# Issuing the two expert weights behind V of batch 0 and V of batch 1 in a fused attention and feed-forward kernel

## The chip, the cores and the metric

The kernel runs on one core of one Trainium2 chip. The metric is the device time of one execution in microseconds (us). A time without a unit below is a point on the profile's time axis, in us from the start of the profiled span.

## The reference

Block-causal attention over 8 batches, 8 heads, 576 positions and head dimension 64 is followed by a feed-forward layer whose gate is `h * sigmoid(beta * h)`. All inputs and the output are float32.

```python
scores = q @ k.T / sqrt(64)                       # per batch and head, 576 x 576
scores = where(block_i >= block_j, scores, -1e9)  # blocks of 64 positions
attn = softmax(scores) @ v                        # 576 x 64
x = attn, heads side by side                      # 4608 x 512
h = x @ w_in                                      # w_in 512 x 2048
g = h * 1 / (1 + exp(-beta * h))
out = g @ w_out                                   # w_out 2048 x 512
```

## The kernel before

The kernel is written as a list of operations with dependencies, buffers and assumed durations. At build time a planner (`Plan.schedule`) plays this list through a model of the engines and writes down one fixed order for each engine; on the chip every engine works through its order and stops at an instruction whose semaphores have not come yet. The assumed durations (`xfer` of a DMA, `LAND` until a DMA counts as landed) and the priorities (`prio`, smaller first) set only the order. The dependencies (`deps`) become real waits.

**Attention.** A unit is one pair of heads of one batch, four units per batch. Q and K of a unit are loaded into staging buffers `ST` (six of them), cast to bf16 on POOL (`QKn`, two buffers, L493 for batches 0 and 1, L532 later) and transposed into `QKT` (three buffers): on the tensor engine PE for batches 0 and 1 (L502, copied out at L510), by DMA afterwards (L539). The score products are at L561 and their exponentials are taken on ACT (L569, L581) into `E` (three buffers). V of a whole batch is loaded into `Vs` (two buffers), cast on POOL to `Vn` (L447), and multiplied with E at L605, thirty matmuls per unit, called PV below. The result is divided by its sums on DVE (L617, L624) and transposed into `xT` (L649 and L659 or L657 up to batch 4, by DMA at L637 from batch 5).

**Feed-forward.** Nine row blocks of 512 rows, called row 0 to row 8. For each of 16 groups j, four matmuls at L695 (`w_in`) fill a PSUM bank, ACT takes a tanh (L705) and DVE forms `gT` (L709). Then L726 (`w_out`) sums over the 16 groups for four slices of the block, and ACT writes them out. For row 0 the first three slices are split into four parts, each needing only a quarter of w_out. `w_in` and `w_out` are each loaded in four pieces: 1 MB of float32 is read and 512 KB of bf16 is written, so these DMAs cast.

**Queues.** Q, K and V are issued on SP (queue q1 in the profile). The weights are issued on POOL between its casts (queue q0). All transfers run on the same 16 DMA engines.

**What held the weights and loads in this version** is a short block near the end: w_in piece 0 waits for Q and K of unit 3, the other pieces also for the second half of V of batch 0; w_out waits for Q and K of unit 6; and the Q and K of units 4 to 7 wait for w_in piece 1 to land.

```python
for i, w in enumerate(win):
    w.deps += [ld["Q", 3], ld["K", 3]] + (ld["V", 0, 4] if i else [])
for w in wout:
    w.deps += [ld["Q", 6], ld["K", 6]]
for u in range(4, 8):
    for o in [ld["Q", u], ld["K", u]] + (ld["V", 1, 0] if u == 4 else []):
        o.deps += [win[1]]
```

Of the kernel before, what the change touches and what calls it, by code (L numbers as in the profile page):

```python
# [9 lines left out]
B, H, S, D = 8, 8, 576, 64  # L10
# [19 lines left out]
class Op:  # L30
    def __init__(self, engs, dur, lat, emit, deps, tiles, prio, mode, dma, xfer):
        self.xfer = xfer
        self.engs, self.dur, self.lat, self.emit = engs, dur, lat, emit
        self.deps, self.tiles, self.prio, self.mode, self.dma = list(deps), tiles, prio, mode, dma
        self.eng = None
        self.start = self.end = None
        self.order = None
        self.need = False
        self.tick = None
        self.after = None  # L40
        self.lazy = False
        self.fill = 0


class Plan:
# [4 lines left out]
    SLACK = 120.0  # L50
    LAND = 2000.0
    BACKLOG = 4000.0
# [22 lines left out]
    def schedule(self):  # L75
# [17 lines left out]
        order = {e: [] for e in engs}  # L93
        now, nsched, rings = 0.0, 0, 0.0
        import heapq
        events = [0.0]
        pend = []
# [18 lines left out]
        fill = [o for o in self.ops if o.fill]  # L116
        while nsched < len(self.ops) - len(fill) or pend:
            if not events:
                raise RuntimeError("the plan has no way on")
            now = heapq.heappop(events)  # L120
            while pend and pend[0][0] <= now + 1e-9:
                _, _, o = heapq.heappop(pend)
# [20 lines left out]
            while progress:  # L143
                progress = False
                for e in engs:
# [4 lines left out]
                    for o in pool:  # L150
# [5 lines left out]
                        if o.after is not None and o.after.start is None:  # L156
                            continue
                        if o.lazy and rings > now + self.BACKLOG:
                            heapq.heappush(events, rings - self.BACKLOG + 1)
                            continue  # L160
# [50 lines left out]
                    heapq.heappush(pend, (o.end, o.idx, o))  # L211
                    heapq.heappush(events, o.end)
                    heapq.heappush(events, eng_free[e])
# [75 lines left out]
def bass_blockwise_causal_attn__then__act_swish_beta_kernel(  # L289
# [10 lines left out]
    with es:  # L300
# [97 lines left out]
        for a in range(4):  # L398
            def fwi(g, e, a=a):
                n = slice(512 * a, 512 * a + 512)  # L400
                return [g.dma_start(w_in[:, :, n], moe_w_in[:, n].rearrange("(c p) n -> p c n", p=128))]

            win.append(P.op("POOL", 1000, fwi, xfer=3400, dma=(f"d_win{a}", 1), prio=-19))
        for a in range(4):
# [3 lines left out]

            wout.append(P.op("POOL", 1000, fwo, xfer=3400, dma=(f"d_wout{a}", 1), prio=-18))

# [14 lines left out]
        for b in range(B):  # L425
            ts, t = P.tile("Vs"), P.tile("V")
            tl[b] = t
            for h0, h1 in ([(0, 4), (4, 8)] if b == 0 else [(0, 8)]):
                vs = []
                for i in range(6):  # L430
                    def fv(g, e, ts=ts, b=b, h0=h0, h1=h1, i=i):
                        if i < 4:
# [38 lines left out]
        for u in range(NU):  # L471
# [8 lines left out]
            if b < QB:  # L480

                turned = []
                for w, (nm, src) in enumerate((("Q", q), ("K", k))):
# [5 lines left out]

                    o = ld[nm, u] = P.op("SP", 420, fl, tiles=[ts], xfer=1200, prio=u, dma=["d_S", 0, 1])  # L490

# [324 lines left out]
```

## Time and profile before

| | |
|---|---|
| median of 3 runs | 376.37 us (375.22 to 379.33) |
| the profiled execution | 380.57 us, its span 378.8 us |
| PE busy | 345.8 us, 91% of the span |
| ACT, DVE, POOL busy | 212.3, 163.2, 75.9 us |
| read from and written to HBM | 36.71 MB and 9.44 MB |
| mean granted clock of PE | 0.963 |

The profiled execution is 1.77 us longer than its span and 4.2 us longer than the median run. PE is the engine with the most work, so time is to be looked for where PE stands still: a wait of another engine counts only where PE waits for it in turn. In the timelines an entry gives start, length, engine, line and operation, and in square brackets the idle time ahead of it with what ended it. An engine name ending in q (SPq) is its queue of DMA issues: the length is that of the issue, not of the transfer.

### The profile page before, as it was taken

The page shows a single profiled execution, that of the slowest core. Times are in us where ns is not written, and L with a number is a line of the kernel's source. Part 1 is how long each engine was busy: PE and PEld are TensorE (multiplying, and loading weights), DVE is VectorE, ACT ScalarE, POOL GpSimd, SP SyncE. Part 2 cuts the span into 40 slices and gives each one's busy share as a digit, 9 for nine tenths or more (in the row PEclk, how much of TensorE's full clock was granted, in tenths as well). Part 3 has the DMA queues.
Part 4 walks back from the last instruction along what each step waited for, and adds up shares of the span by engine and source line. Part 5 has one row for each costly group of instructions (what it writes and reads, how often), then busy time and mean ns, then how long its engine had stood idle before and what let it go on. Part 6 is the DMA issues. An engine that isn't in the chain of part 4 may idle for free.

```text
span 378.8 us, 6727 instructions
## 1 busy us (share of the span) xinstructions
PE 345.8 (91%) x2728; PEld 171.7 (45%) x2728; DVE 163.2 (43%) x367; ACT 212.3 (56%) x314; POOL 75.9 (20%) x105
## 2 busy tenths in 40 slices
PE   7779923999899799999999999999999999999986
PEld 4454403544354454454544544444554444444432
DVE  4556921416522365523864137314740750740710
ACT  2847840317934759647897189519932841742821
POOL 6451804323242241053003120400000000000000
PEclk9899985999999689999999999999999999999999
DMA  8969999989989987699066899870121002001002
GB/s 213 183 106 240 212 211 191 186 208 249 207 193 230 191 193 163 139 226 235 3 137 149 186 194 172 179 154 29 32 61 60 25 3 80 29 28 55 29 29 83
DMA packets 146527, 52.03 MB, mean 137 GB/s; under 512 B 134704, under 2 KB 141888, under 8 KB 146496
## 3 DMA queue, kind: packets, MB, share of 16 engines
q1 hardware_dynamic: 137088, 37.97, 49.3%
q10 hardware_dynamic: 5184, 9.44, 7.1%
q0 software_dynamic: 4224, 4.19, 7.0%
q8 instruction: 21, 0.34, 0.4%
q14 instruction: 10, 0.08, 0.1%
HBM read 36.71 MB, written 9.44 MB: 122 GB/s over the span
## 4 chain that ended last, share of the span: by engine, by line
PE 64%; SPq 7%; ACT 6%; DMA 3%; DVE 2%; issue 1%
PE PS L726 28%; PE PS L695 25%; PE PS L605 6%; SPq L521 4%; PE PS L561 4%; ACT E L569 3%; SPq L637 2%; ACT th L705 2%; DMA QKT<-QKn 2%; PE PS L649 2%; DVE gT L709 1%; DMA xT<-xq 1%; SPq L524 1%; SPq L436 0%; DVE xq L624 0%
## 5 line engine op out<-in xcount | busy, mean ns | idle before, releaser
L695 PE MATMUL PS<-xT,w_in 128*128 128x512 bf16 x576 | 133.7, 382 | 0.6 <-DVE gT L709 0.5
L709 DVE SCALAR_TENSOR_TENSOR gT<-th,PS 128x512 bf16<-128x512 f32 x144 | 97.5, 684 | 78.5 <-ACT th L705 77.9
L726 PE MATMUL PS<-w_out,gT 128*128 128x512 bf16 x576 | 128.4, 380 | 2.2 <-DVE gT L709 2.2
L705 ACT ACTIVATE th<-PS,beta 128x512 f32<-128x512 f32 x144 | 98.4, 700 | 24.6 <-PE PS L695 24.5
L569 ACT ACTIVATE E<-PS 128x1024 bf16<-128x1024 f32 x96 | 95.8, 1044 | 20.0 <-PE PS L561 19.7
L726 PEld LDWEIGHTS PS<-w_out,gT 128*128 128x128 bf16 x576 | 54.8, 98 | 69.0 <-DVE gT L709 3.2
L695 PEld LDWEIGHTS PS<-xT,w_in 128*128 128x128 bf16 x576 | 52.7, 98 | 65.8 <-issue 5.1
L737 ACT ACTIVATE ost<-PS 128x512 f32<-128x512 f32 x36 | 21.5, 597 | 97.5 <-PE PS L726 97.5
L605 PE MATMUL PS<-Vn,E 128*128 128x65 bf16 x960 | 37.9, 201 | 16.2 <-POOL Vn L447 14.9
L561 PE MATMUL PS<-QKT 64*128 64x512 bf16 (+5 forms) x384 | 40.6, 290 | 7.5 <-ACT E L569 5.5
L605 PEld LDWEIGHTS PS<-Vn,E 128*128 128x128 bf16 x960 | 35.7, 103 | 23.7 <-POOL Vn L447 13.4
L532 POOL CAST QKn<-ST 128x640 bf16<-128x640 f32 x48 | 34.7, 722 | 49.2 <-DMA ST<-in_k_dram 25.4
L447 POOL CAST Vn<-Vs 128x2560 bf16<-128x2560 f32 (+1 forms) x9 | 18.8, 2084 | 105.9 <-DMA Vs<-in_v_dram 105.9
L561 PEld LDWEIGHTS PS<-QKT 64*128 64x128 bf16 (+1 forms) x384 | 13.7, 96 | 31.1 <-issue 9.7
L624 DVE TENSOR_TENSOR xq<-PS,inv 128x640 bf16<-128x640 f32 x32 | 26.3, 822 | 0.9
L617 DVE RECIPROCAL inv<-PS 128x10 f32<-128x10 f32 x32 | 7.0, 219 | 44.5 <-PE PS L605 44.3
L575 DVE MEMSET E<- 64x64 uint32 x64 | 7.2, 112 | 38.0 <-ACT E L569 36.5
L659 DVE COPY xT<-PS 128x64 bf16<-128x64 bf16 (+2 forms) x40 | 9.6, 286 | 15.9 <-PE PS L649 15.8
L581 ACT ACTIVATE E<-PS 128x64 bf16<-128x64 f32 x32 | 7.0, 251 | 16.5 <-PE PS L561 14.9
L493 POOL CAST QKn<-ST 96x768 bf16<-96x768 f32 x14 | 11.6, 827 | 13.7 <-DMA ST<-in_q_dram 10.2
L510 DVE COPY QKT<-PS 128x576 bf16<-128x576 bf16 x16 | 12.0, 755 | 3.2 <-PE PS L502 2.7
L577 DVE MEMSET E<- 64x128 uint32 x32 | 5.3, 165 | 14.5 <-ACT E L569 13.6
(31 smaller groups left out, 57.1 us busy)
## 6 DMA issues: line engine op xcount, KB each, us to landing
out_dram<-ost ACTq DMA_DIRECT2D x36, 256.0 KB, 2.3
Vs<-in_v_dram SPq DMA_DIRECT2D x28, 256.0 KB, 4.2
ST<-in_q_dram SPq DMA_DIRECT2D x48, 128.0 KB, 2.9
ST<-in_k_dram SPq DMA_DIRECT2D x48, 128.0 KB, 2.9
ST<-in_q_dram SPq DMA_DIRECT2D x8, 288.0 KB, 6.2
ST<-in_k_dram SPq DMA_DIRECT2D x8, 288.0 KB, 6.5
w_in<-in_moe_w_in_dram POOLq DMA_DIRECT2D x4, 512.0 KB, 7.9
w_out<-in_moe_w_out_dram POOLq DMA_DIRECT2D x4, 512.0 KB, 9.6
```

The source lines that it names most:

```text
L447: return g.tensor_copy(Vn[t.slot][:, :, h0:h1, 0:64], Vs[ts.slot][:, :, h0:h1, :])
L521: z = [g.dma_start(ST[ts.slot][:, i, :, :], src[b, h, 128 * i:128 * i + 128, :].rearrange("h p d -> p h d")) for i in range(4)]
L532: return g.tensor_copy(QKn[tn.slot][:].rearrange("p a w n -> p (a w n)")[:, 640 * (2 * a + w):][:, 0:640] .rearrange("p (t h d) -> p t h d ...
L561: z = g.matmul(o, QKT[tqk.slot][r, p, 1, 128 * t:128 * t + m], QKT[tqk.slot][r, p, 0, q0:q1])
L569: return g.activation(E3[te.slot][:, g0, :, :], PS[:, ps.slot:ps.slot + 2, :], ACT.Exp, scale=0.125)
L605: z = g.matmul(o, eblk(te, t, i, h), Vn[Tv.slot][:, t, 2 * c + h, 0:65], start=(t == 0), stop=(t == i))
L624: return g.tensor_tensor(xq[tx.slot][:].rearrange("p i (h d) -> p h i d", h=2), both(pv, 0, 64), x, ALU.mult)
L695: z = g.matmul(PS[:, ph.slot, :], w_in[:, c, 128 * j:128 * j + 128], xT[:, c, row % RX:row % RX + RC], start=(c == 0), stop=(c == 3))
L705: return g.activation(th[tt.slot][:], PS[:, ph.slot, :], ACT.Tanh, scale=beta[:, j:j + 1])
L709: return g.scalar_tensor_tensor(out=gT[tg.slot][:, j, :], in0=th[tt.slot][:], scalar=1.0, in1=PS[:, ph.slot, :], op0=ALU.add, op1=ALU.mult)
L726: z = g.matmul(PS[:, po.slot, :], gT[tg.slot][:, j, 128 * w:128 * w + 128], w_out[:, j, :], start=(j == 0), stop=(j == NJ - 1))
L737: return g.activation(ost[to.slot][:], PS[:, po.slot, :], ACT.Copy, scale=0.5)
```

## The change

The weights' dependencies are replaced: all four pieces of w_in wait for the second half of V of batch 0, all four pieces of w_out wait for V of batch 1, and Q and K of units 4 to 7 and V of batch 1 wait for no weight any more. The priorities of the weights on POOL change with that, so that the first two pieces of w_in and the first of w_out are issued ahead of the cast that waits for the same V. The planner's model of the DMAs changes from one ring with a fixed time per transfer to two rings (`H` for SP and ACT, `S` for POOL) that share the engines packet by packet when both hold work; assumed transfer times and the landing time change too. This model runs at build time and acts on the chip only through the orders.

```diff
+        self.pkt = 22.0
...
-    LAND = 2000.0
+    LAND = 2600.0
+    PKT, BOTH = 97.0, 0.87
...
+        rings, left, clock = {"H": [], "S": []}, {"H": 0.0, "S": 0.0}, 0.0
+        told = None
+
+        def speeds():
+            if rings["H"] and rings["S"]:
+                h = rings["H"][0].pkt
+                return {"H": h / (self.BOTH * (h + self.PKT)), "S": self.PKT / (self.BOTH * (h + self.PKT))}
+            return {"H": 1.0, "S": 1.0}
+
+        def flow(till):
+
+            nonlocal clock, told
+            while True:
+                v = speeds()
+                z = [(max(clock, round(clock + rings[k][0].todo / v[k], 3)), k) for k in rings if rings[k]]
+                t, k = min(z, default=(1e18, None))
+                d = min(t, till) - clock
+                for x in rings:
+                    if rings[x]:
+                        rings[x][0].todo -= d * v[x]
+                        left[x] -= d * v[x]
+                clock += d
...
+                o = rings[k].pop(0)
+                o.end = clock + self.LAND
...
-                        if o.lazy and rings > now + self.BACKLOG:
-                            heapq.heappush(events, rings - self.BACKLOG + 1)
+                        if o.lazy and left["H"] > self.BACKLOG:
                             continue
...
                     if o.dma is not None:
-                        rings = max(rings, start + 700) + o.xfer
-                        o.end = rings + self.LAND
+                        x = "S" if e == "POOL" else "H"
+                        rings[x].append(o)
+                        left[x] += o.xfer
+                        o.todo = o.xfer
+                        flow(now)
...
-            win.append(P.op("POOL", 1000, fwi, xfer=3400, dma=(f"d_win{a}", 1), prio=-19))
+            win.append(P.op("POOL", 1000, fwi, xfer=3150, dma=(f"d_win{a}", 1), prio=-50 if a < 2 else -32))
...
-            wout.append(P.op("POOL", 1000, fwo, xfer=3400, dma=(f"d_wout{a}", 1), prio=-18))
+            wout.append(P.op("POOL", 1000, fwo, xfer=3150, dma=(f"d_wout{a}", 1), prio=-18 if a < 1 else 4.6))
...
-                                   xfer=1400 * n, prio=3.5 + 0.1 * (h0 > 0) if b == 0 else 4 * b + (3.5 if b < 2 else 0.5),
+                                   xfer=1580 * n, prio=3.5 + 0.1 * (h0 > 0) if b == 0 else 4 * b + (3.5 if b < 2 else 0.5),
...
-                    o = ld[nm, u] = P.op("SP", 420, fl, tiles=[ts], xfer=1200, prio=u, dma=["d_S", 0, 1])
+                    o = ld[nm, u] = P.op("SP", 420, fl, tiles=[ts], xfer=1050, prio=u, dma=["d_S", 0, 1])
+                    o.pkt = 80.0
...
-        for i, w in enumerate(win):
-            w.deps += [ld["Q", 3], ld["K", 3]] + (ld["V", 0, 4] if i else [])
+        for w in win:
+            w.deps += ld["V", 0, 4]
         for w in wout:
-            w.deps += [ld["Q", 6], ld["K", 6]]
-        for u in range(4, 8):
-            for o in [ld["Q", u], ld["K", u]] + (ld["V", 1, 0] if u == 4 else []):
-                o.deps += [win[1]]
+            w.deps += ld["V", 1, 0]
```

What this does to the orders is shown at three places. The changed file is longer: its L439, L444, L485, L600, L644, L731 and L762 are the old L401, L406, L447, L561, L605, L695 and L726.

The first place is POOL around the loads of w_in, from the last cast of a Q or K of batch 0 (`ST1`) to the first of batch 1 (`ST2`). Before:

```order
L493 CAST QKn1<-ST1 96x768 [waits s_POOL,s_d_S1_0]
L401 DMA w_in<-in_moe_w_in_dram 128x4x512 [waits s_d_S0_0]
L447 CAST Vn0<-Vs0 128x5x4x64 [waits s_POOL,s_d_V0_0]
L447 CAST Vn0<-Vs0 128x5x4x64 [waits s_POOL,s_d_V0_4]
L401 DMA w_in<-in_moe_w_in_dram 128x4x512 x3
L454 MEMSET ST0 64x256 [waits s_POOL]
```

Now:

```order
L532 CAST QKn1<-ST1 96x768 [waits s_POOL,s_d_S1_0]
L485 CAST Vn0<-Vs0 128x5x4x64 [waits s_POOL,s_d_V0_0]
L439 DMA w_in<-in_moe_w_in_dram 128x4x512 [waits s_d_V0_4]
L439 DMA w_in<-in_moe_w_in_dram 128x4x512
L485 CAST Vn0<-Vs0 128x5x4x64 [waits s_POOL]
L439 DMA w_in<-in_moe_w_in_dram 128x4x512 x2
L532 CAST QKn0<-ST2 96x768 [waits s_PE,s_d_S2_0,s_POOL]
```

Piece 0 of w_in has moved behind both halves of V of batch 0 (semaphores `s_d_V0_0` and `s_d_V0_4`), and two issues now stand ahead of the second cast; the memsets of ST have moved down.

The second place is POOL around w_out and the cast of V of batch 1 (`Vn1<-Vs1`). Before:

```order
L493 CAST QKn1<-ST1 96x768 [waits s_POOL,s_d_S1_0]
L406 DMA w_out<-in_moe_w_out_dram 128x4x512
L493 CAST QKn1<-ST2 96x768 [waits s_POOL,s_d_S2_0]
L493 CAST QKn1<-ST3 96x768 [waits s_d_S3_0,s_POOL]
L406 DMA w_out<-in_moe_w_out_dram 128x4x512 x3
L447 CAST Vn1<-Vs1 128x40x64 [waits s_POOL,s_d_V1_0]
```

Now:

```order
L532 CAST QKn1<-ST2 96x768 [waits s_d_S2_0,s_POOL]
L492 MEMSET ST3 64x256 [waits s_POOL]
L492 MEMSET ST4 64x256 [waits s_POOL]
L492 MEMSET ST5 64x256 [waits s_POOL]
L532 CAST QKn1<-ST3 96x768 [waits s_d_S3_0,s_POOL]
L444 DMA w_out<-in_moe_w_out_dram 128x4x512 [waits s_d_V1_0]
L485 CAST Vn1<-Vs1 128x40x64 [waits s_POOL]
L444 DMA w_out<-in_moe_w_out_dram 128x4x512 x3
```

The whole of w_out has moved behind the landing of V of batch 1 (`s_d_V1_0`), three pieces also behind its cast.

The third place is PE at the start of row 1, where the first scores of batch 2 come in (`QKT1`). Before:

```order
L726 MATMUL PS<-w_out,gT0 128x512 x36
L695 MATMUL PS<-xT,w_in 128x512 x56
L561 MATMUL PS<-QKT1 128x512 x2
L561 MATMUL PS<-QKT1 128x448 x2
L561 MATMUL PS<-QKT1 128x64 x2
L561 MATMUL PS<-QKT1 64x64 x4
L695 MATMUL PS<-xT,w_in 128x512 x8
```

Now:

```order
L762 MATMUL PS<-w_out,gT0 128x512 x40
L731 MATMUL PS<-xT,w_in 128x512 x36
L600 MATMUL PS<-QKT1 128x512 x2
L600 MATMUL PS<-QKT1 128x448 x2
L600 MATMUL PS<-QKT1 128x64 x2
L600 MATMUL PS<-QKT1 64x64 x4
L731 MATMUL PS<-xT,w_in 128x512 x4
```

The scores of batch 2 have moved 20 matmuls of row 1 forward. The order of Q, K and V on SP is the same as before up to batch 2; what is gone there is the wait of unit 4's Q for w_in.

More of the change, by code (lines that the diff above doesn't have):

```diff
@@ L93, in schedule @@
         order = {e: [] for e in engs}
-        now, nsched, rings = 0.0, 0, 0.0
+        now, nsched = 0.0, 0
+        rings, left, clock = {"H": [], "S": []}, {"H": 0.0, "S": 0.0}, 0.0
[17 more added lines that the diff above has]
+                clock += d
+                if t > till:
+                    if k and told != t:
+                        told = t
+                        heapq.heappush(events, t)
+                    return
+                o = rings[k].pop(0)
+                o.end = clock + self.LAND
+                heapq.heappush(pend, (o.end, o.idx, o))
+                heapq.heappush(events, o.end)
         import heapq
@@ L116, in schedule @@
         fill = [o for o in self.ops if o.fill]
-        while nsched < len(self.ops) - len(fill) or pend:
+        while nsched < len(self.ops) - len(fill) or pend or rings["H"] or rings["S"]:
             if not events:
@@ L205, in schedule @@
                     if o.dma is not None:
-                        rings = max(rings, start + 700) + o.xfer
-                        o.end = rings + self.LAND
+                        x = "S" if e == "POOL" else "H"
+                        rings[x].append(o)
+                        left[x] += o.xfer
+                        o.todo = o.xfer
+                        flow(now)
                     eng_free[e] = start + o.dur
@@ L210, in schedule @@
                     nsched += not o.fill
-                    heapq.heappush(pend, (o.end, o.idx, o))
-                    heapq.heappush(events, o.end)
+                    if o.dma is None:
+                        heapq.heappush(pend, (o.end, o.idx, o))
+                        heapq.heappush(events, o.end)
                     heapq.heappush(events, eng_free[e])
```

## The prediction

> **What bounds the kernel now.** I read the page first, then the waits of the first 130 us, then the timelines of PE, POOL and SP there, then the busy time by stage.
>
> ```profile
> PE 345.8 (91%) x2728; PEld 171.7 (45%) x2728; DVE 163.2 (43%) x367; ACT 212.3 (56%) x314; POOL 75.9 (20%) x105
> ...
> PE PS L605 <- POOL Vn L447: 14.9, 2, 13.2
> ```
>
> PE is idle for 378.8 - 345.8 = 33 us. The second row (total, times, longest, up to 130 us) has the largest single part of it: one wait of 13.2 us for a cast of V. The timeline of PE shows its place, POOL's what held the cast:
>
> ```profile
> 49.28 0.39 PE L561 MATMUL PS<-QKT 64*128 64x320 bf16 x4 [0.26 <-ACT E L569]
> 62.84 3.48 PE L605 MATMUL PS<-Vn,E 128*128 128x65 bf16 x60 [13.17 <-POOL Vn L447]
> 66.45 1.40 PE L726 MATMUL PS<-w_out,gT 128*128 128x512 bf16 x4
> ...
> 42.40 0.75 POOL L406 DMA_DIRECT2D w_out<-in_moe_w_out_dram  x1
> 44.91 2.23 POOL L406 DMA_DIRECT2D w_out<-in_moe_w_out_dram  x3
> 60.47 2.32 POOL L447 CAST Vn<-Vs 128x2560 bf16<-128x2560 f32 x1 [13.33 <-DMA Vs<-in_v_dram]
> ```
>
> PE has run out of work at 49.67, and V of batch 1 is in only at about 60.4; its cast lasts 2.32. The four w_out pieces were issued just ahead, although their first user (L726) stands behind that PV. The DMA engines were shared meanwhile:
>
> ```profile
> q0 software_dynamic: 2064, 2.05, 83.9%
> q1 hardware_dynamic: 4049, 1.01, 36.9%
> ```
>
> These are the queues from 45 to 60 (packets, MB, share of 16 engines): w_out on q0 moved twice the bytes of V on q1. By stage (length, PE busy, PEld, DVE, ACT, POOL, clock, DMA share, GB/s):
>
> ```profile
> 50.00:63.00 13.00, 0.15 (x3) 0.16 (x4) 0.80 (x3) 1.63 (x2) 2.41 (x2) 0.64 1.09 193
> 98.00:134.00 36.00, 31.61 (x314) 16.79 (x311) 11.50 (x39) 21.36 (x31) 10.42 (x10) 0.88 0.95 202
> 134.00:200.00 66.00, 64.80 (x616) 32.97 (x614) 36.43 (x97) 48.75 (x73) 13.88 (x17) 0.99 0.71 156
> 200.00:278.00 78.00, 76.59 (x665) 36.77 (x664) 33.82 (x81) 51.16 (x77) 13.31 (x14) 1.00 0.64 132
> ```
>
> From 134 on PE is about 98% busy while the DMA share falls to 0.7. Up to 63 DMA is the limit, afterwards PE. So time saved before 63 should last, if the loads of batches 2 and 3 keep up.
>
> **The change, part by part.** *V of batch 0.* Rows of POOL, SP and PE:
>
> ```profile
> 21.80 1.26 POOL L447 CAST Vn<-Vs 128x1280 bf16<-128x1280 f32 x1 [5.81 <-DMA Vs<-in_v_dram]
> 23.00 2.23 POOL L401 DMA_DIRECT2D w_in<-in_moe_w_in_dram  x3
> ...
> 14.96 1.76 SPq L436 DMA_DIRECT2D Vs<-in_v_dram  x2
> 66.90 3.10 SPq L436 DMA_DIRECT2D Vs<-in_v_dram  x2
> 71.88 2.32 POOL L447 CAST Vn<-Vs 128x2560 bf16<-128x2560 f32 x1 [4.73 <-DMA Vs<-in_v_dram]
> ...
> 23.20 1.07 PE L605 MATMUL PS<-Vn,E 128*128 128x65 bf16 x30 [1.78 <-POOL Vn L447]
> 28.18 9.67 PE L695 MATMUL PS<-xT,w_in 128*128 128x512 bf16 x44 [0.15 <-ACT xT L657]
> ```
>
> V of batch 0 was issued by 16.72 and in at about 21.8, with a piece of w_in beside it. V of batch 2, with no weight beside it, was in 1.88 after its last issue (70.00 to 71.88). So V of batch 0 should be in at 18.6. Two issues of 0.74 (a third of 2.23) now stand ahead of the cast, which ends at 18.6 + 1.5 + 1.26 = 21.4 instead of 23.06: 1.7 earlier. PV and then row 0's L695 move from 28.18 to 26.5. Piece 0 of w_in leaves at 18.6:
>
> ```profile
> w_in<-in_moe_w_in_dram POOLq DMA_DIRECT2D x1, 512.0 KB, 7.6
> ```
>
> Before, it landed 7.6 after its issue (window 13 to 14), now at 26.2: in time. The eight Q and K casts on POOL and the transposes of unit 4 on PE start earlier, among the same work.
>
> *V of batch 1.* SP's wait for w_in piece 1 goes. It had held Q and K of unit 4, and V of batch 1 behind them:
>
> ```profile
> SPq L487 <- DMA w_in<-in_moe_w_in_dram: 12.7, 1, 12.7
> ...
> 29.39 0.34 SPq L487 DMA_DIRECT2D ST<-in_q_dram  x1
> ...
> q0 software_dynamic: 608, 0.60, 122.9%
> ...
> q1 hardware_dynamic: 555, 0.79, 104.1%
> ...
> q1 hardware_dynamic: 2794, 0.70, 121.2%
> ```
>
> The last three rows give the rate of each load nearly alone, over 3 us each: w_in (27 to 30), Q and K (33 to 36), V (66 to 69). Ahead of V's landing there now are eight Q and K pieces of 0.295 MB, 2.36 MB at 0.263 MB/us = 9.0 us; w_in, 2.10 MB as written at 0.20 = 10.5; and V itself, 1.18 MB at 0.233 = 5.1. Mixing neither costs nor gains: 45 to 60 moved 2.05 / 0.20 + 1.01 / 0.233 = 14.6 us worth in 15. The sum, 24.6, starts when V of batch 0 leaves the engines, near 17.5, so it ends at 42.1 and V is in at 44.0 with the 1.88 above. One w_out issue (0.75) and the cast end it at 47.1. The bounds are 42 (no landing delay) and 47 (a tenth slower).
>
> PE's work between 28.18 and 49.67 is 21.5 us, the same work in another order; from 26.5 it lasts until 48.0. So V no longer holds PE, with 0.9 to spare, and PV starts at 48.0 instead of 62.84: **-14.8**. At the upper bound the cast ends at 50.1 and PE waits 2.
>
> *The clock.* PV of two units took 3.48 after the wait; a unit took 0.90 later:
>
> ```profile
> 74.68 0.90 PE PS L605 x30
> ```
>
> The granted clock of 50 to 63 was 0.64. Without the wait it is 3.48 - 1.80 = **-1.7**. [...]
>
> *w_out behind V.* This is the wait that the change adds. Behind it on POOL stand the cast of V and the casts of batch 2.
>
> ```profile
> w_out<-in_moe_w_out_dram POOLq DMA_DIRECT2D x2, 512.0 KB, 7.7
> ...
> w_out<-in_moe_w_out_dram POOLq DMA_DIRECT2D x3, 512.0 KB, 10.8
> ...
> 85.38 12.25 PE L695 MATMUL PS<-xT,w_in 128*128 128x512 bf16 x56
> ```
>
> Landing took 7.7 (issues of 42 to 45) to 10.8 (45 to 48). Piece 0 leaves at 44.0 and is in at 51.7. L726 came 3.6 after PV's start (62.84 to 66.45), 1.9 at full clock; with 0.6 of scores and transposes ahead of it now, it wants piece 0 at 50.5: **+1.2**, bounds 0 and 4.3. The other pieces leave after the cast, at 47.1, and land at 54.8, 58.4 and 62.0 (15 us for four pieces, as above). By its order PE wants them near 56.6, 60.5 and 63.1, so these waits are hidden, by 1 to 2 us. Row 1 then starts at 85.38 - 14.8 - 1.7 + 1.2 = 70.1.
>
> *Batches 2 and 3.* Batch 2's scores stand 20 matmuls earlier in row 1 (4.4 us at 12.25 / 56 each).
>
> ```profile
> 72.99 3.38 SPq L539 DMA_TRANSPOSE QKT<-QKn  x1
> 114.01 5.05 SPq L539 DMA_TRANSPOSE QKT<-QKn  x1
> ...
> QKT<-QKn SPq DMA_TRANSPOSE x12, 5.7
> ...
> 97.56 0.79 PE L561 MATMUL PS<-QKT 64*128 64x512 bf16 x10
> 102.53 0.39 PE L561 MATMUL PS<-QKT 64*128 64x448 bf16 x4 [1.81 <-ACT E L569]
> 143.31 0.79 PE L561 MATMUL PS<-QKT 64*128 64x512 bf16 x10
> ```
>
> Batch 2's first scores move from 97.56 to 97.56 - 15.3 - 4.4 = 77.9. Their transpose was in at 72.99 + 5.7 = 78.7. All loads up to w_out are now through at 17.5 + 24.6 + 10.25 = 52.4 instead of about 60, so those behind come some 8 earlier: 70.7, in time. Batch 3's second pair was in at 114.01 + 5.7 = 119.7 and wanted at 143.31; with 12 matmuls of row 2 fewer ahead of it (2.6 us) it is wanted at 143.31 - 15.3 - 2.6 = 125.4, or 5 sooner: in time even if it comes no earlier. From 98 to 134 PE idled 4.4 us and had a cold stretch (clock 0.88), most of it waiting for exponentials (the row of 102.53) that are bunched at the end of row 1. Spread over more of row 1 they may give up to 5 back. Loads that come no earlier cost 0.8 (78.7 against 77.9); loads held up by one more w_out piece (3.6) cost 4.4, say 5. The nearest rows, those after 134, have almost no idle time. I take a small gain, **-1.5**, since the last unit's chain still ends the row.
>
> **Sum:** -14.8 - 1.7 + 1.2 - 1.5 = -16.8, against the profiled execution's 380.57: 363.8. That execution is 4.2 above the median of 376.37, so the same gain gives **359.6**.
>
> **Rivals.** *The wait moves to w_out* (V is there, w_out is not): piece 0 at 10.8 costs 4.3, and later pieces each as late again some 3 more. 363 to 367. For it: 0.9 to 2 us of slack everywhere. Against it: less stands in q1 beside w_out then. [...]
>
> *Batches 2 and 3 come late,* because w_out now runs beside their loads: up to 5 us, 364 to 368. Against it: the 8 us above.
>
> *V of batch 1 gains nothing and w_out is late too* (the slower side). w_in would hold V up as w_out did. This decides from V's landing at 60 on, where PE waits as before and w_out piece 0 lands at 60.4 + 7.7 = 68.1 instead of being there at 66.45, the last at 60.4 + 3.1 + 7.7 + 3 x 3.6 = 82, wanted at about 79: +1.7 and +1 to 2 more, 380. Against it: 24.6 us of loads would have to last 42.
>
> *Nothing changes,* since the planner's model is no event on the chip and the weights would only trade places with Q and K: 373 to 379. Against it: the orders show w_in and w_out behind V.
>
> **How the numbers follow.** Forecast 0.61 (355 to 363), w_out 0.16, batches 2 and 3 0.12, nothing 0.05, slower 0.06. Low end: no wait for w_out (-1.2) and 5 back in row 1 (-3.5 more), 354.9, so 354.5. High end: V 2 late, w_out 3.1 more, loads 5, 369.7, so 369.5. Runs of this kernel differ by about 1%, so 1% is the bound of no change: faster 0.89, same 0.05, slower 0.06.
>
> **What would show it.** The wait of PE for Vn at L644 under 2 us instead of 13.17; the cast of batch 1's V starting near 45; row 0's L731 near 26.5; granted clock 1.0 from 48 to 60; row 1 near 70. I am wrong if PE waits at L762 for w_out over 4 us, at L600 for batch 2 or 3, or at L644 beyond 50.

## The result, and the profile after

| | before | changed |
|---|---|---|
| median | 377.85 us (375.22 to 381.85, 4 runs) | 358.48 us (358.10 to 359.54, 4 runs) |
| the profiled execution, its span | 380.57, 378.8 us | 358.74, 356.9 us |
| mean granted clock of PE in it | 0.963 | 0.995 |

The ratio is 0.951 (0.944 to 0.959). It leaves out the slow run of 381.85 us, which is over 1.5% above the fastest run of the kernel before; without it the median before is 376.37. The forecast was 359.6.

The engines' row of the page after, and two of the three waits up to 130 us in which the weights take part (total, times, longest; the third, POOL's w_in behind V of batch 0, is 3.0):

```profile
PE 334.9 (94%) x2679; PEld 168.0 (47%) x2721; DVE 163.2 (46%) x367; ACT 210.8 (59%) x314; POOL 75.9 (21%) x105
```

```profile
POOL w_out L444 <- DMA Vs<-in_v_dram: 9.7, 1, 9.7
PEld PS L762 <- DMA w_out<-in_moe_w_out_dram: 1.1, 2, 0.6
```

The row that carried the argument before, PE waiting 14.9 us for `Vn`, has no successor: the wait now stands on POOL, in front of w_out, and what PE's side waits for w_out is 1.1. (49 matmul records are missing on PE here, so its busy time is somewhat more than 334.9.) The timelines of POOL and PE:

```profile
19.02 1.63 POOL L439 DMA_DIRECT2D w_in<-in_moe_w_in_dram  x2 [2.99 <-DMA Vs<-in_v_dram]
20.62 1.28 POOL L485 CAST Vn<-Vs 128x1280 bf16<-128x1280 f32 x1
...
44.31 0.75 POOL L444 DMA_DIRECT2D w_out<-in_moe_w_out_dram  x1 [9.72 <-DMA Vs<-in_v_dram]
45.05 2.33 POOL L485 CAST Vn<-Vs 128x2560 bf16<-128x2560 f32 x1
47.30 2.23 POOL L444 DMA_DIRECT2D w_out<-in_moe_w_out_dram  x3
68.49 2.32 POOL L485 CAST Vn<-Vs 128x2560 bf16<-128x2560 f32 x1 [7.03 <-DMA Vs<-in_v_dram]
```

```profile
29.23 0.81 PE L731 MATMUL PS<-xT,w_in 128*128 128x512 bf16 x3 [0.64 <-DVE QKT L549]
29.97 0.75 PE L600 MATMUL PS<-QKT 64*128 64x512 bf16 x8
...
41.39 7.08 PE L731 MATMUL PS<-xT,w_in 128*128 128x512 bf16 x31
48.30 0.27 PE L454 MATMUL PS<-identF,identB 128*128 128x256 bf16 x1
48.41 1.97 PE L644 MATMUL PS<-Vn,E 128*128 128x65 bf16 x60
...
52.58 0.81 PE L762 MATMUL PS<-w_out,gT 128*128 128x512 bf16 x3 [0.77 <-ACT E L608]
...
70.69 7.93 PE L731 MATMUL PS<-xT,w_in 128*128 128x512 bf16 x35
...
115.30 1.67 PE L731 MATMUL PS<-xT,w_in 128*128 128x512 bf16 x7 [0.16 <-DVE inv L656]
```

V of batch 1 is in by 44.31 (60.4 before), its cast ends at 47.38, and PE comes to the PV only at 48.41, out of its own work. Row 2 began here in the timeline before:

```profile
133.51 2.86 PE L695 MATMUL PS<-xT,w_in 128*128 128x512 bf16 x8
```

With these starts the two spans divide into four stretches:

| stretch | before | after | gain | forecast |
|---|---|---|---|---|
| to PV of batch 1 | 62.84 | 48.41 | 14.4 | 14.8 |
| PV to row 1 | 22.54 | 22.28 | 0.3 | 0.5 |
| row 1 to row 2 | 48.13 | 44.61 | 3.5 | together 1.5 |
| row 2 to the end | 245.29 | 241.60 | 3.7 | |

The third stretch by stage, before and then after (length, PE, PEld, DVE, ACT, POOL, clock, DMA share, GB/s):

```profile
85.40:133.50 48.10, 43.71 (x371) 22.09 (x369) 19.71 (x51) 30.60 (x44) 13.31 (x14) 0.91 1.01 213
```

```profile
70.70:115.00 44.30, 40.09 (x366) 20.17 (x369) 19.18 (x50) 29.79 (x44) 13.95 (x18) 1.00 1.04 221
```

PE idles 4.4 us in one (48.10 - 43.71) and 4.2 in the other, where five matmul records are missing. Before, PE ran at half clock from 125.26 to 135.50 (granted clock 0.50). Thirty PV matmuls took 1.83 us there (126.47) and 1.07 ahead of it (120.89); PE's work is longer in it, and so waits are hidden. What the order did in row 1 is read further down, from a kernel with the old orders and full clock. By the mean clock, this half-clock stretch is not in every run. Of 39 runs of the kernel before that were taken beside the experiments, 17 had a mean clock below 0.9675 and a median of 379.15 us, the other 22 had 376.70. The profiled one, with 0.963, belongs to the first group. From it to 0.977, the highest of these clocks, is, by an estimate, 10.6 us less at half clock (0.014 x 378.8 / 0.5), about the length of that stretch; those runs left no trace to see it in. So the gain of 21.8 between the two profiled executions is 17.9 between the medians 376.37 and 358.48, and 19.4 from 377.85.

### The profile page after: what moved, and what is told of

The parts are those of the page before. It is cut to its first block, busy times and chain, and to the rows that moved or that the text cites. A ratio compares the mean times of both kernels' runs of the same rounds, so it can differ in the third digit from the quotient of the medians.

```text
span 356.9 us, 6674 instructions
## 1 busy us (share of the span) xinstructions
PE 334.9 (94%) x2679; PEld 168.0 (47%) x2721; DVE 163.2 (46%) x367; ACT 210.8 (59%) x314; POOL 75.9 (21%) x105
## 4 chain that ended last, share of the span: by engine, by line
PE 71%; SPq 8%; ACT 6%; DMA 6%; DVE 4%; issue 2%; POOL 2%; POOLq 0%
PE PS L762 34%; PE PS L731 26%; SPq L471 6%; PE PS L644 6%; PE PS L600 4%; ACT E L608 3%; DMA w_out<-in_moe_w_out_dram 3%; DVE gT L745 3%; ACT th L741 2%; SPq L474 2%; DMA ST<-in_k_dram 1%; DMA ST<-in_q_dram 1%; POOL Vn L485 1%; PE PS L688 1%; POOL QKn L532 1%
## 5 line engine op out<-in xcount | busy, mean ns | idle before, releaser
L731 PE MATMUL PS<-xT,w_in 128*128 128x512 bf16 x548 | 129.2, 380 | 4.9 <-DVE gT L745 1.4
L762 PE MATMUL PS<-w_out,gT 128*128 128x512 bf16 x562 | 126.1, 379 | 3.6 <-DVE gT L745 1.5
L762 PEld LDWEIGHTS PS<-w_out,gT 128*128 128x128 bf16 x576 | 54.9, 98 | 68.6 <-DVE gT L745 2.2
L731 PEld LDWEIGHTS PS<-xT,w_in 128*128 128x128 bf16 x576 | 52.2, 98 | 66.1 <-issue 4.7
L600 PE MATMUL PS<-QKT 64*64 64x64 bf16 (+5 forms) x384 | 38.0, 282 | 4.5 <-ACT E L608 2.4
L644 PEld LDWEIGHTS PS<-Vn,E 128*128 128x128 bf16 x960 | 33.5, 99 | 8.6 <-ACT E L608 1.8
L644 PE MATMUL PS<-Vn,E 128*128 128x65 bf16 x960 | 35.1, 196 | 1.8 <-ACT E L608 1.0
L485 POOL CAST Vn<-Vs 128x2560 bf16<-128x2560 f32 (+1 forms) x9 | 18.8, 2087 | 77.3 <-DMA Vs<-in_v_dram 77.3
L600 PEld LDWEIGHTS PS<-QKT 64*128 64x128 bf16 (+1 forms) x384 | 13.4, 96 | 28.1 <-issue 9.1
L688 PE MATMUL PS<-identB,xq 128*128 128x128 bf16 (+1 forms) x100 | 10.5, 216 | 0.5 <-DVE xq L663 0.4
```

The lines of the kernel that those rows point to most:

```text
L485: return g.tensor_copy(Vn[t.slot][:, :, h0:h1, 0:64], Vs[ts.slot][:, :, h0:h1, :])
L600: z = g.matmul(o, QKT[tqk.slot][r, p, 1, 128 * t:128 * t + m], QKT[tqk.slot][r, p, 0, q0:q1])
L644: z = g.matmul(o, eblk(te, t, i, h), Vn[Tv.slot][:, t, 2 * c + h, 0:65], start=(t == 0), stop=(t == i))
L731: z = g.matmul(PS[:, ph.slot, :], w_in[:, c, 128 * j:128 * j + 128], xT[:, c, row % RX:row % RX + RC], start=(c == 0), stop=(c == 3))
L762: z = g.matmul(PS[:, po.slot, :], gT[tg.slot][:, j, 128 * w:128 * w + 128], w_out[:, j, :], start=(j == 0), stop=(j == NJ - 1))
```

## The experiments

All times are medians against the kernel before on the same chip, unless another comparison is named. "V in" is the time at which V of batch 1 has landed.

### The waits alone, every order as before

The first kernel moves w_out on POOL behind the landing of V of batch 1 and changes nothing else.

```diff
+        def move(ws, early, cast, vs):
...
+                w.deps = list(vs)
...
+        move(wout, 1, load[4], ld["V", 1, 0])
```

One piece stands ahead of the cast of V, three stand behind it.

> The kernel before with all its orders on PE, ACT, DVE and SP kept word for word; only w_out is moved on POOL, piece 0 just ahead of the cast of V of batch 1 and pieces 1 to 3 just behind it, waiting for that V. Theory A (V was held up by w_out sharing the DMA engines): V's 1.18 MB go alone from about 45 and land at 51.3 instead of 60.4, the cast ends at 54.4, PV starts there instead of 62.84 (-8.4, a little of the cold clock -0.8), and PE then waits about 2 us for piece 0 of w_out; 369.5 us against 376.4. Theory B (the orders of the planner make the gain, the waits alone move nothing): 376 us.

Measured: 372.62 us (371.98 to 374.43), ratio 0.986 (0.978 to 0.993). PE's timeline:

```profile
52.14 2.83 PE L605 MATMUL PS<-Vn,E 128*128 128x65 bf16 x60 [2.81 <-POOL Vn L447]
...
56.59 1.49 PE L726 MATMUL PS<-w_out,gT 128*128 128x512 bf16 x3 [1.43 <-DMA w_out<-in_moe_w_out_dram]
...
76.28 12.25 PE L695 MATMUL PS<-xT,w_in 128*128 128x512 bf16 x55
```

V is in at 49.0, 2.3 ahead of the estimate. PV comes 10.7 earlier, row 1 9.1 earlier, and a price of 1.4 for w_out appears. The median falls by 6.2 (378.83 to 372.62), so the waits move something without any new order on PE.

The second moves w_in behind V of batch 0 and drops the wait of Q, K and V of batch 1 for w_in. w_out stays early.

```diff
+        move(win, 2, load[2], ld["V", 0, 4])
+        for u in range(4, 8):
+            for o in [ld["Q", u], ld["K", u]] + ld["V", 1, 0]:
+                o.deps = [d for d in o.deps if d is not win[1]]
```

> The kernel before with all its orders on PE, ACT, DVE and SP kept; only w_in is moved on POOL behind V of batch 0 (two pieces ahead of the cast of its second half, two behind), and the waits of units 4 to 7 for w_in piece 1 are gone. w_out is issued where it was, after the casts of units 6 and 7, ahead of V of batch 1. Theory A: V of batch 1 queues with all of w_in and w_out and lands near 17.5 + 24.6 + 10.5 + 1.9 = 54.5, PV starts at 57 instead of 62.84, w_out is there: 370 us. Theory B: 376 us.

Measured: 375.57 us (372.46 to 376.82), ratio 0.991 (0.986 to 0.995). POOL, then PE:

```profile
56.70 2.32 POOL L447 CAST Vn<-Vs 128x2560 bf16<-128x2560 f32 x1 [18.09 <-DMA Vs<-in_v_dram]
```

```profile
30.82 10.79 PE L695 MATMUL PS<-xT,w_in 128*128 128x512 bf16 x43 [2.31 <-DMA w_in<-in_moe_w_in_dram]
...
59.08 3.48 PE L605 MATMUL PS<-Vn,E 128*128 128x65 bf16 x60 [5.64 <-POOL Vn L447]
...
82.00 12.25 PE L695 MATMUL PS<-xT,w_in 128*128 128x512 bf16 x55
```

V comes 3.7 earlier only, since w_out (issued at 32 to 38 here) is still in its way, and PE now waits 2.3 for w_in. Both came out worse than estimated: V at 56.7 and not 54.5, the time 375.57 and not 370.

The third has both edits.

> The kernel before with all its orders on PE, ACT, DVE and SP kept, and all three changes of waits (w_in behind V of batch 0, no wait of SP for w_in, w_out behind V of batch 1). Theory A: V of batch 1 is in at 44 as in the changed kernel; PE's old order has 44 matmuls of row 0 ahead of the first transposes of batch 1 and so waits for the pieces of w_in, PV starts near 51.6 instead of 48.4 in the changed kernel; 363.5 us, most of the gain. Theory B: 374 us or more, since the orders were not made for it.

Measured: 366.55 us (364.87 to 367.50), ratio 0.968 (0.959 to 0.977).

```profile
45.48 2.33 POOL L447 CAST Vn<-Vs 128x2560 bf16<-128x2560 f32 x1
```

```profile
41.73 0.75 PE L561 MATMUL PS<-QKT 64*128 64x512 bf16 x8
...
52.72 3.40 PE L605 MATMUL PS<-Vn,E 128*128 128x65 bf16 x60 [2.10 <-ACT E L569]
...
74.76 12.25 PE L695 MATMUL PS<-xT,w_in 128*128 128x512 bf16 x55
```

V is in as early as in the changed kernel, the cast ends at 47.8, and PE still starts PV at 52.72: it waits for exponentials. In the old order the scores that they need stand behind 52 matmuls of w_in (44, 4 and 4) and begin at 41.73; in the new order they begin at 29.97 (timeline after, above). So the waits bring V, and the old order can use only 10 of the 14 us.

### The orders alone

The changed kernel's planner with the old waits and priorities:

```diff
...
-        for w in win:
-            w.deps += ld["V", 0, 4]
+        for i, w in enumerate(win):
+            w.deps += [ld["Q", 3], ld["K", 3]] + (ld["V", 0, 4] if i else [])
         for w in wout:
-            w.deps += ld["V", 1, 0]
+            w.deps += [ld["Q", 6], ld["K", 6]]
+        for u in range(4, 8):
+            for o in [ld["Q", u], ld["K", u]] + (ld["V", 1, 0] if u == 4 else []):
+                o.deps += [win[1]]
```

> The changed kernel's planner model with the waits and priorities of the kernel before (w_in behind Q and K of unit 3, w_out behind those of unit 6, SP waits for w_in piece 1). Its order on PE has 64 matmuls of row 0 with w_out ahead of the PV that waits for V of batch 1. Theory A: V of batch 1 still lands at 60.4, but PE fills the wait with row 0's w_out as its pieces land (49.4 to 59.9), PV starts near 66 and row 1 near 73 instead of 85.4: 364 us, nearly the whole gain by order alone. Theory C (only an earlier V helps): 375 us.

Measured: 368.77 us (367.77 to 370.15), ratio 0.975 (0.967 to 0.983).

```profile
60.31 2.32 POOL L485 CAST Vn<-Vs 128x2560 bf16<-128x2560 f32 x1 [13.06 <-DMA Vs<-in_v_dram]
```

```profile
60.05 6.22 PE L765 MATMUL PS<-w_out,gT 128*128 128x512 bf16 x27 [0.60 <-DMA w_out<-in_moe_w_out_dram]
66.10 1.97 PE L644 MATMUL PS<-Vn,E 128*128 128x65 bf16 x60
...
78.03 6.29 PE L734 MATMUL PS<-xT,w_in 128*128 128x512 bf16 x23 [1.01 <-DVE xT L698]
```

V is as late as before (its landing is no matter of the model), but the new model knows it and puts w_out's matmuls of row 0 ahead of PV, so that PE works while V comes. This is the mechanism of theory A, with PV at 66.10 as forecast, but row 1 begins at 78.03 and not at 73: the orders alone are worth 10 us (378.83 to 368.77), and not nearly the whole gain. Theory C fails.

The counterpart keeps the old model and has the new waits and priorities:

> The changed waits and priorities, but the orders written by the old planner model. V of batch 1 should be in near 44 and row 1 start between 71 and 75, as in the changed kernel or in the frozen orders with all waits. If the new waits let either model write a good order (theory W), the time is within 3 us of the changed kernel, 358 to 362, and row 1 to the end lasts 286 to 288. If the new model is worth its own 8 us on top of the waits, as the step from frozen orders with all waits (366.6) to the changed kernel suggests (theory M), 365 to 368.

Measured: 362.57 us (362.08 to 362.93), ratio 0.964 (0.960 to 0.968). PE's timeline:

```profile
49.17 1.97 PE L605 MATMUL PS<-Vn,E 128*128 128x65 bf16 x60
```

PV starts within a microsecond of the changed kernel's. The result lies just above the first expectation (358 to 362) and clearly below the second. What planning anew with the old model gives over the old orders is not clear of the noise: 0.964 (0.960 to 0.968) here, 0.968 (0.959 to 0.977) there. The new model gives 3 us more by the medians on this chip (362.57 and, below, 359.58) and 5 by the ratios (0.964 and 0.950).

### The wait on w_out, undone in the new orders

The changed kernel once more, beside the next kernels:

> The changed kernel once more, on the chip of the next three kernels, to compare them with. Expected 357.5 to 360, granted clock 0.989 to 0.995 in every run, no half-clock stretch behind 25 us.

Measured: 359.58 us (358.21 to 361.46), ratio 0.950 (0.943 to 0.958). The profiled run, 361.46, was the slowest of the four, and shows where the expectation was wrong:

```profile
29.70 1.49 PE L731 MATMUL PS<-xT,w_in 128*128 128x512 bf16 x3 [2.61 <-DMA w_in<-in_moe_w_in_dram]
...
50.97 1.97 PE L644 MATMUL PS<-Vn,E 128*128 128x65 bf16 x60
...
72.17 7.93 PE L731 MATMUL PS<-xT,w_in 128*128 128x512 bf16 x35
```

PE waited 2.6 us for piece 0 of w_in, a half-clock stretch began in that wait (0.50 from 28.37 to 35.20), and PE came to PV 2.6 later although V was in at 43.96.

Now every order of the changed kernel, with w_out early:

```diff
+        q = P.order["POOL"]
+        i = q.index(wout[0])
+        for n, w in enumerate(wout):
+            q.remove(w)
+            w.deps = [ld["Q", 6], ld["K", 6]]
...
+        q[i:i] = wout
```

On POOL the four issues now stand behind the last cast of Q and K of batch 1 and ahead of the cast of V.

> The changed kernel's order on PE, ACT, DVE and SP unchanged, but the wait on w_out undone: all four pieces wait only for Q and K of unit 6 again and stand on POOL ahead of the cast of V of batch 1, behind the last cast of Q and K of batch 1. They leave near 35 to 38 instead of 44 to 49. If the prediction's sharing holds (45 to 60 in the kernel before: q0 took 70% of the engines' time beside q1), V of batch 1 has some 2 to 2.5 us of work left when w_out starts on the queue near 40, needs 7 to 8 us for it, and is in at 49 to 51 instead of 44.0; PV of batch 1 starts at 52.5 to 54.5 instead of 48.4 with a half-clock stretch behind the wait, w_out is never waited for, and the time is 4 to 6 us above the changed kernel: 362.5 to 364.5. If the new orders carry the gain by themselves and the wait is not needed: within 1 us of the changed kernel.

Measured: 368.73 us (367.95 to 369.61), 9.2 above the changed kernel on the same chip. POOL, then PE:

```profile
34.87 2.97 POOL L444 DMA_DIRECT2D w_out<-in_moe_w_out_dram  x4
55.94 2.32 POOL L485 CAST Vn<-Vs 128x2560 bf16<-128x2560 f32 x1 [18.10 <-DMA Vs<-in_v_dram]
```

```profile
58.31 3.48 PE L644 MATMUL PS<-Vn,E 128*128 128x65 bf16 x60 [8.84 <-POOL Vn L485]
...
81.34 7.93 PE L731 MATMUL PS<-xT,w_in 128*128 128x512 bf16 x35
```

This isolates the wait: the same instructions in the same order on PE, ACT, DVE and SP, and V lands 12 us later (55.94 against 43.96), because w_out stands beside it on the engines. The expectation had the direction and half the size (V at 49 to 51). The queues from 40 to 54 show why:

```profile
q0 software_dynamic: 2045, 2.03, 85.2%
q1 hardware_dynamic: 3028, 0.76, 35.6%
```

By the prediction's rates that is 10.2 us of w_out and 3.3 us of V: V had more left than the 2 to 2.5 us assumed, and got 24% of the time instead of 30%, so nearly all of w_out (2.03 MB) passed ahead of V's end. The early issue costs 9.2 us, because V, which is wanted sooner, stands on the other queue.

### The clock of PV

The kernel before, with dummy matmuls while PE waits for V of batch 1, so that PV meets the full clock:

```diff
+            if pre is not None:
+                pre(eng)
...
+            if u == 4:
+                def warmup(g, pv=pv):
+                    for i in range(100):
+                        g.matmul(PS[:, pv.slot, 0:256], identB[:], identW)
...
+                av.pre = warmup
```

The wait for the cast stands behind the dummies. The second kernel has 75 of them.

> The kernel before with its orders and waits, and 100 dummy matmuls of 128x256 on PE while it waits for the cast of V of batch 1, into the PSUM banks that the PV behind them overwrites (work added, none left out). It measures the clock's part of the gain by itself. The wait stays 13 us, filled. If the clock term of the prediction (-1.7) is right, the 60 PV matmuls last 1.8 to 2.0 instead of 3.48, row 1 starts 1.5 to 2 earlier, and the time is 1.5 to 2 us below the kernel before (377 instead of 378.8). Rival 1: the half-clock stretch near 125 to 135 hangs on the earlier one and goes too; then 4 to 6 us are gained. Rival 2: the dummies only move the cold stretch elsewhere: within 0.5 us of before.

Measured with 100: 377.04 us (374.28 to 380.52), ratio 0.999 (0.995 to 1.004). This miss was the experiment's own: the dummies ended at 63.6, the cast at 61.0, so PV waited 2.6 us for them.

> The warm-up of the earlier run with 75 dummy matmuls instead of 100: there PV waited 2.6 us for the dummies themselves (they ended at 63.6, the cast of V at 61.0), which hid what was looked for. With 75 they end near 60.6, ahead of the cast's end at 61 to 63. PV of two units then lasts 1.97 (as in the earlier run) instead of 3.48, row 1 starts 1.5 earlier, and if the clock term of the prediction is right the time is 1 to 2 us below the kernel before at equal granted clock elsewhere. If the cold clock costs nothing on the path: within 0.5 us of it.

Measured with 75: 376.15 us (373.80 to 377.57), ratio 0.994 (0.990 to 0.997), 2.0 us less than before.

```profile
51.41 10.03 PE L622 MATMUL PS<-identF,identB 128*128 128x256 bf16 x75 [2.01 <-ACT E L576]
61.68 1.98 PE L612 MATMUL PS<-Vn,E 128*128 128x65 bf16 x60 [0.24 <-POOL Vn L454]
```

PV takes 1.98 instead of 3.48 in the same order: the clock term is shown, at 1.5 of the 1.7 forecast. The granted clock was 0.50 from 62.84 to 66.32 in the kernel before, and 1.00 from 63 to 70 with 100 dummies, where PV took 1.97 as well. (V was in 1.1 earlier in this profiled run, so the start of row 1 is not compared.) The earlier half-clock stretch, 13.65 us in the kernel before (0.50 from 53.58 to 67.23), is about 3.4 with 100 dummies, by an estimate from the clock of 0.87 from 50 to 63 ((1 - 0.87) x 13 / 0.5). The one near 125 does not hang on its length: it is there with 100 dummies (0.51 from 126.00 to 136.40) and with 75, where thirty PV matmuls took 1.83 at 125.08 and at 129.81 and 1.07 or 1.08 before (119.50) and after (135.28).

### Where w_out could stand

w_out later, behind K of unit 8:

```diff
-            w.deps += ld["V", 1, 0]
+            w.deps += ld["V", 1, 0] + [ld["K", 8]]
```

> The changed kernel with one more wait: w_out also waits for K of unit 8 (in near 60 now), so all four pieces leave near 60 instead of 44 to 49, behind two casts of batch 2. It builds the rival that the wait moves to w_out. V of batch 1 should still be in at 44 and PV start near 48.4. If w_out is needed where the prediction put it, the first w_out matmul waits until 67 to 70 against 52.6 before, filled in part by some 6 us of scores and transposes moved ahead: PE waits 8 to 14 us at it, half clock behind the wait, time 366 to 372. If the planner can fill the gap (w_out is not near the critical path), within 2 us of the changed kernel, 358 to 361.

Measured: 361.00 us (360.13 to 362.72), ratio 0.961 (0.956 to 0.965). With nothing of w_out beside it K of unit 8 was in at 49.6, not 60, so the pieces left 3.1 to 5.3 late instead of 12 to 15, and the one wait on PE is this:

```profile
57.93 3.07 PE L762 MATMUL PS<-w_out,gT 128*128 128x512 bf16 x7 [1.06 <-DMA w_out<-in_moe_w_out_dram]
```

The planner had put other work ahead. Lateness of this size costs 1.4 us against the changed kernel's 359.58 and 2.5 against its 358.48, and the intervals of the ratios overlap, so the cost is not clear of the noise. A w_out at 60 was not tested, nor was this lateness in a fixed order; what the rival that the wait moves to w_out would cost there is not shown.

w_out earlier, behind the first three of the six pieces of V of batch 1, three issues ahead of the cast:

> The changed kernel, but w_out waits only for the first three of the six pieces of V of batch 1, and three of its issues stand ahead of the cast. It closes the gap of the DMA queues at 42 to 46 that comes from issuing w_out only when V has landed. w_out leaves 1.5 to 3 us earlier and lands 2 to 3 earlier (50, 55, 58, 62), V lands up to 1 later (44 to 45), its cast starts 1.5 later behind the issues, and the PV at 49.5 to 50.5 with 1 to 2 us of wait. The loads of batch 2 come 1 to 2 earlier. If batch 2 and w_out have slack in the changed kernel, as its trace shows, the time stays the same or gets up to 1.5 us worse (358 to 360); if the queue gap still costs time, it is 1 to 2 us better (356.5 to 357.5).

Measured: 360.39 us (357.74 to 360.52), ratio 0.956 (0.950 to 0.962). POOL, then PE:

```profile
42.41 2.23 POOL L444 DMA_DIRECT2D w_out<-in_moe_w_out_dram  x3 [7.82 <-DMA Vs<-in_v_dram]
```

```profile
69.33 7.93 PE L731 MATMUL PS<-xT,w_in 128*128 128x512 bf16 x35
```

w_out leaves 1.9 earlier, the 1.1 of waiting for it are gone, and row 1 starts 1.4 earlier. But row 1 then ran into half clock (0.50 from 110.38 to 117.20); the one run of four with a clock of 0.995 took 357.74, the others, with 0.981, 360.35 to 360.52. So no gain is shown over the changed kernel.

Only piece 0 of w_out early, behind Q and K of unit 7:

> The changed kernel, but piece 0 of w_out waits only for Q and K of unit 7 instead of V of batch 1 (planned anew: 12 matmuls of w_out stand ahead of PV of batch 1 then). One piece of 1 MB is now in front of V: at 0.20 MB/us as written that is at most 2.6 us for V, in at 45 to 46.6 instead of 44.0, cast done at 48 to 49.7. The 12 w_out matmuls (2.6 us) cover that. Theory: the time stays within 1.5 us of the changed kernel (357.5 to 360), since PE has the same work in another order; the PE waits of 1.1 us at w_out go. Rival: every weight byte ahead of V costs its full time at PV: 361 to 362.

Measured: 362.91 us (360.80 to 363.49), 3.3 above the changed kernel on the same chip, which is beyond both expectations. V is in at 47.5, 3.6 later. PE fills this with w_out's matmuls and begins row 1 at 72.22, as the changed kernel beside it does (72.17). V of batch 2 is cast 5.8 later (73.33 against 67.58); whether that costs anything is not shown. The profiled runs differ by 1.1 of span only, so most of the 3.3 is not placed.

### What the kernels say together

For the kernels in which row 1's w_in matmuls begin only when row 0's w_out matmuls are done, from their timelines and granted clock (us):

| kernel | V in | PV | row 1 | row 1 to the end | half clock in that part |
|---|---|---|---|---|---|
| before | 60.4 | 62.84 | 85.38 | 293.4 | 10.2 |
| w_out wait, old orders | 49.0 | 52.14 | 76.28 | 293.9 | 13.7 |
| w_in edit, old orders | 56.7 | 59.08 | 82.00 | 292.7 | 10.2 |
| all waits, old orders | 44.7 | 52.72 | 74.76 | 290.5 | 0 |
| 75 dummies, old orders | 59.3 | 61.68 | 82.30 | 293.4 | 13.7 |
| 100 dummies, old orders | 58.7 | 63.58 | 84.19 | 294.1 | 13.7 |
| new model, old waits | 60.3 | 66.10 | 78.03 | 287.9 | 2.3 |
| w_out behind three pieces of V | by 44.6 | 48.45 | 69.33 | 289.3 | 6.8 |
| piece 0 of w_out early | 47.5 | 53.55 | 72.22 | 288.6 | 3.4 |
| changed, w_out early | 55.9 | 58.31 | 81.34 | 286.5 | 0 |
| changed | 44.3 | 48.41 | 70.69 | 286.2 | 0 |
| changed, again | 44.0 | 50.97 | 72.17 | 287.5 | 3.4 |

The last two columns divide the rest of the gain, with one profiled run of each kernel. In the same order, what follows row 1's start does not depend on when it starts (286.5 from 81.34, 286.2 from 70.69). It depends on the order, 4.3 us (290.5 to 286.2, no half clock in either), and on the half clock, about 2.9 (290.5 to 293.4; the five kernels with the old orders and a half clock lie 2.2 to 3.6 above 290.5). So of the 21.8 between the profiled executions 14.7 is the start of row 1, for which waits and orders are both needed (74.76 and 78.03 with one, 70.69 with both), about 4.3 the order behind it, and about 2.9 a half-clock stretch. Behind row 1's start PE idles 12.9 us in the changed kernel (286.21 - 273.34) and 16.4 with all waits in the old orders (290.54 - 274.18), which covers 3.5 of the 4.3.

Row 1 by itself, up to the start of row 2, with all waits in the old orders:

```profile
74.76:121.18 46.42, 40.46 (x368) 20.58 (x371) 19.74 (x51) 30.62 (x45) 12.40 (x15) 1.00 1.04 227
```

At full clock the old order idles 6.0 us in it, the new one 4.4 (70.69 to 115.30, 44.61 long with PE busy for 40.24). So the order gives 1.8 in row 1 and 2.5 behind it, and the half clock lengthened row 1 of the kernel before by 1.7 (46.42 to 48.13). From 70 to 121 PE waits 3.8 us for exponentials in the old order and 1.9 in the new.

## Why the prediction was right

The bound was right, and so was the mechanism: the loads ahead of V held it up, and PE with it. That the total came within 1.1 us (359.6 against 358.48) is in part luck, since the errors of the last two points below nearly cancel. By its steps:

- **V of batch 0 and w_in.** V in at 18.6: 19.0 by POOL's row. The cast's end at 21.4: 21.90. The step that failed is the landing of w_in piece 0, put at 7.6 after its issue and in time. It landed 9.9 after its issue, near 28.9, and row 0's w_in matmuls began at 29.23 instead of 26.5. In the profiled run scores and transposes filled this; in the second profiled run, and twice in the old orders, PE waited 1.8 to 2.6 us. The 7.6 came from a piece that had less beside it: q1 carried 0.70 MB from 13 to 21 in the kernel before, and 1.85 MB from 19 to 29 in the changed one.
- **V of batch 1.** In at 44.0: 44.3. The sum of the loads' rates held, and closer than its bounds of 42 and 47 promised (a tenth slower comes to 46.4, not 47); in the experiments like estimates of this landing were off by 0.7, 2.2 and 2.3 us, and by 5 to 7 with w_out early. Cast done at 47.1: 47.4. PV at 48.0, PE's own work the limit by 0.9: at 48.41, by 1.0. That this hung on the order, too, the prediction took for granted in "the same work in another order"; with the old order it would have been 52.7.
- **The clock, -1.7:** PV lasts 1.97 instead of 3.48 (granted clock 1.00 from 48.41 to 50.40, 0.50 before), and the dummies show the same 1.5 without the change.
- **w_out, +1.2:** first used at 52.58, 1.1 of waits in all. Row 1 at 70.1: 70.69.
- **Loads of batch 2 8 us earlier:** wrong. V of batch 2 is cast from 68.49 instead of 71.88, 3.4 earlier, and the transposes of unit 8 and its neighbour started 2.7 earlier, at 70.30 instead of 72.99. w_out, now issued only at V's landing, moves beside these loads: from 44 to 64 the two queues carried 2.10 and 1.81 MB,

```profile
q0 software_dynamic: 2109, 2.10, 66.2%
q1 hardware_dynamic: 7271, 1.81, 47.6%
```

  which is two thirds and a half of the engines' time. Up to 46 the weights' queue was all but empty (4 packets from 44 to 46), and from 46 to 47 both queues together ran at only 50 to 87 GB/s; the sum left this gap out. It cost nothing: the transpose landed 5.5 after its issue, at 75.8, and the scores that need it began at 78.55.
- **Row 1 and behind, -1.5:** the mis-sized term. It measured -7.2 between the profiled executions. The reason given, exponentials spread over row 1, holds with about the size given: 1.8 in row 1 against the old order at full clock. In the kernel before, the half clock hides it, since PE's idle time there is nearly the same. What the term left out is 2.5 that the order gives from row 2 on, where the prediction saw almost no idle time, and about 2.9 of half clock, of which it named the place and claimed little.
- **From the profiled execution to the median.** The prediction took the same gain off the median. By the mean clocks, more than half of the runs have less half clock than the profiled execution, so part of what it lost was no part of the median. This error and the one above are of opposite sign and nearly cancel: 16.8 was forecast, 21.8 lies between the profiled executions, and 17.9 between the medians 376.37 and 358.48.

Of the rivals, "the wait moves to w_out" did not come: PE's side waits 1.1 us for w_out, about the 1.2 that the forecast had, and not 4.3 and more. Batch 2 was in time, and V of batch 1 came 16 us earlier and not as late as before. The rival that nothing changes was wrong in its reason as well: the new model's orders are worth 10 us by themselves.

## What to carry to other kernels

When two queues share the DMA engines, as q0 and q1 did here (85.2% and 35.6% of the engines' time with w_out early), rank the transfers by when the compute engine wants them and hold a large later one behind the landing of an urgent one; the sum of bytes over measured rates forecast that landing to 0.3 us here; like estimates for the other kernels missed by 0.7 to 2.3 us, and one by 5 to 7. Then plan the order for the new landing times: the same waits gave 12 us in the old orders, and the change with its own orders 18 to 19. Compare the orders at equal clock: here a half clock hid 1.6 us of waiting in row 1 (6.0 to 4.4). Before subtracting a gain seen in one profiled execution from a median, see from the granted clock whether that execution is a typical one.

## What was not expected of the hardware

Some half-clock stretches came without any long gap in PE's work: in the 3.41 us ahead of the two below, its longest single wait was 0.67 us (up to 123.13) and 0.91 us (up to 108.01). PE's busy time in 3.41 us before and during such stretches, in the kernel before and in the one with w_out behind the third piece of V:

```profile
121.85:125.26 3.41, 2.07 (x25) 0.81 (x21) 1.79 (x6) 2.94 (x5) 0.00 (x0) 1.00 1.20 244
125.26:135.50 10.24, 9.00 (x88) 5.10 (x89) 3.55 (x13) 6.23 (x8) 2.32 (x1) 0.50 0.84 175
```

```profile
106.97:110.38 3.41, 1.92 (x40) 1.19 (x38) 0.95 (x7) 2.83 (x4) 1.14 (x2) 1.00 1.01 255
110.38:117.20 6.82, 5.69 (x49) 3.17 (x51) 2.86 (x9) 4.15 (x5) 2.89 (x4) 0.50 1.02 208
```

and the same length in the changed kernel and with all waits in the old orders, where the clock stayed full afterwards:

```profile
109.56:112.97 3.41, 2.15 (x43) 1.49 (x45) 1.43 (x5) 2.61 (x4) 1.68 (x3) 1.00 1.16 240
```

```profile
90.10:93.50 3.40, 1.59 (x10) 0.72 (x11) 1.56 (x4) 3.40 (x5) 0.00 (x0) 1.00 1.29 235
```

The two half-clock stretches here last 10.24 and 6.82 us, three and two times 3.41. The length ahead of each had PE busy for 61% and 56%. Seven more lengths ahead of a half clock (0.50) had 66% and 0% (the kernel before, 12.62 to 16.03 and 50.17 to 53.58), 60% (the changed kernel, 13.98 to 17.39), 60% and 52% (the changed kernel, again, 24.96 to 28.37 and 110.29 to 113.70), 56% (w_out behind K of unit 8, 53.90 to 57.32) and 37% (all waits, old orders, 49.10 to 52.50). Of the two lengths above that full clock followed, the first had 63%, the second 47%. So these half clocks followed shares from 0 to 66%, and the share alone did not decide: 63% and 47% brought none. What does was not found. A stretch near 125 in the kernel before is worth some 2 to 3 us (2.9 by the profiled runs, 2.5 between the two groups of the 39).
